# A Fourier mixing kernel: the place of column 128, the queues of the first batch's rows, and the order of the start-up

## The chip, the cores and the metric

The kernel runs on one NeuronCore of a Trainium2 chip. The metric is the device time of one execution in microseconds (us). The core's engines are PE (TensorE, with its weight loads as PEld), DVE (VectorE), ACT (ScalarE), POOL (GpSimd) and SP (SyncE, which here issues DMAs); each runs its own instructions in order and waits for the others by semaphores. DMAs are issued from the queues of SP, ACT and POOL and share 16 DMA engines.

## The reference

```python
def _attn_ref(x):                        # x: 8 batches x 3136 rows x 256 columns
    X = np.fft.fft(x, axis=1)
    X = np.fft.fft(X, axis=2)
    return X.real.astype(np.float32)

def _moe_ref(x, U, V, w_ch1, w_ch2):     # U 3136x32, V 32x3136, w_ch1 256x1024, w_ch2 1024x256
    xt = x.transpose(0, 2, 1)
    h = xt @ U @ V
    u = x + h.transpose(0, 2, 1)
    ch = np.maximum(u @ w_ch1, 0.0) @ w_ch2
    return (u + ch).astype(np.float32)
```

The second function gets the output of the first as its `x`. The kernel multiplies in bf16 and adds up in float32.

## The kernel before

**Folds and tables.** A batch's 3136 rows are loaded as four quarters of 784 rows, each twice: `xr` holds straight rows (`load_r`, a plain DMA), `xf` the rows in reversed order of partitions (`load_f`, an indirect DMA, a gather, from POOL). 98 partitions hold four rows of a quarter each, and one more partition holds row 0 of the quarters (`load_0`). DVE folds them. `along_d` subtracts (part 0) or adds (part 1) column 256 - d to column d, from float32 to bf16, into `EOF_` and `EOR_`; `alone` (POOL) copies the two columns without a partner, 0 and 128. `mirror` then joins straight and reversed rows (`EOS`), `half` makes `GO` (odd rows) and `GE` (even rows) out of that, and `fourth` makes the two `GC` out of `GE`. In these tiles a row has 258 columns of meaning: 0 to 127 are the sine part, 128 to 257 the cosine part. Before the change column 0 of `x` lies at 128, the cosines at 129 to 255, column 128 of `x` at 256, and zeros at 0 and 257. `GO` and `GC` are 384 columns wide (`GW`); `zeros` (POOL) clears 258 to 383 once.

**The transform on PE.** `products` lists matmuls whose weights are 128 columns of `GO` or `GC` (type 0: from column 0; type 1: from column 128) and whose moving operand is a strip of a table of sines or cosines (`TABO`, `TABS`, `TABE`), 196 to 424 columns long. To type 0 come the products of column 128 of `x`: the weights are columns 256 to 383, that is one column of data, the rest zeros. They add into the same PSUM tile. `u_odd` and `u_alone` list the same for the low-rank part, with strips of 32 columns. `seq` and `even_rows` run such a list into a PSUM tile `pt`; `chan`, `first_rows` and `first_u` then transform along the columns with the tables `MSN`, `MC` and `MSX` (a copy of `MSN` with another row 0).

**The network.** `direct` multiplies chunks of 512 rows of the result (`u`) by the first weights, with ReLU on ACT; `mirrors` makes the hidden values of the mirrored rows from those; `second_product` multiplies by the second weights and `store` writes the output. The rows of all batches are taken as 25 such chunks. While a chunk runs, the folds and the transform of a later batch are put between its steps (`due`, `turn`), by hand-written places. Behind L1178 the order of each engine's instructions is pinned for PE and for the folds.

**The start-up.** Up to L1178 the order is written by hand, per engine. POOL makes index rows by iota and issues the gathers. DVE computes phases; ACT makes sines and cosines. `flip_u` turns U's rows round by a matmul with `J`, `fold_u` folds them, and `transform_u` multiplies the folded U by the tables: `odd_k` and `even_k` on PE, into the PSUM tiles `pu`, and `evict` on ACT, which copies the result next to the tables. `filler` gives PE matmuls whose result nobody reads (`fill(n)` of them). The first batch is folded and transformed in two halves, sine and cosine: `half(0, 1, ...)`, `seq(0, 1, 0, ...)`, `seq_both` for the sine half (L1075 to L1087), then the same for the cosine half (L1096 to L1108). Between them POOL's gathers of batch 1 and `places` (the tile `EM`, L283) are issued. `setup.close()` (L1113) gives back the memory of the start-up tiles (`gen`), and the next tile, `u` of `first_u`, takes its place; `lrow`, which `EM` is made from, is among the start-up tiles. `first_u` and `direct(0, 0)` (L1153) follow.

## Time and profile before

| | us |
|---|---|
| median of 3 runs | 437.86 |
| lowest and highest of them | 437.59, 438.01 |
| profiled execution, its own time | 437.52 |
| its span, first instruction to last | 435.7 |
| granted TensorE clock in it | 1.0 |

A profile is one execution. A row of a timeline gives start, duration, engine, line, operation, the tile written and those read, and how many were merged; in brackets the idle time ahead of it and what ended that. A merged row's duration goes from the first start to the last end. Matmuls are pipelined, so one starts long ahead of the end of the one before it, and ends are modelled: for the pace of PE read the starts. `128*8` at a matmul means weights of 128 rows and 8 columns. A row of busy time by stretch has the stretch, its length, then busy time and number for PE, PEld, DVE, ACT and POOL, the granted clock, the share of DMA and GB/s. A row of the chain of waits has start, duration and what ran.

Nearly all instructions of helpers have the helper's line: L453 are folds on DVE, L463 matmuls, L57 gathers.

### The profile page before, as it was taken

What the parts mean: (1) busy time and instruction counts of PE and PEld (TensorE: products, weight loads), DVE (VectorE), ACT (ScalarE), POOL (GpSimd) and SP (SyncE); (2) the same over time, 40 slices, a digit from 0 to 9 for tenths busy, and PEclk for the clock granted to TensorE, in tenths of its full rate; (3) what the DMA queues carried; (4) which work ended last, traced back from release to release, by engine and by line L of the source; (5) the groups of instructions that cost most, each with busy time, mean ns of one, the idle gap of its engine ahead of it and who ended that gap; (6) DMA issues with size and microseconds to landing.
All of it is one profiled execution on the core that took longest, in us unless ns stands there. A gap on an engine that the chain in (4) does not pass through costs nothing.

```text
span 435.7 us, 9397 instructions
## 1 busy us (share of the span) xinstructions
PE 423.2 (97%) x3504; PEld 284.1 (65%) x3504; DVE 319.7 (73%) x665; ACT 291.7 (67%) x633; POOL 128.8 (30%) x340
## 2 busy tenths in 40 slices
PE   5989999999999999999999999999999999999996
PEld 2764667566766766666766766666666766666675
DVE  8988989797898787769777787779867554353442
ACT  7958775666667657776667657776667657765651
POOL 8971323142334223324233232322223101011111
PEclk9999999999999999999999999999999999999999
DMA  7898698868689486837886395866225323334543
GB/s 207 211 212 202 148 284 112 202 160 234 148 162 272 101 210 173 202 74 192 171 208 171 86 232 53 211 164 146 74 80 144 99 74 107 93 122 120 122 125 121
DMA packets 89165, 67.83 MB, mean 156 GB/s; under 512 B 55402, under 2 KB 82430, under 8 KB 89118
## 3 DMA queue, kind: packets, MB, share of 16 engines
q1 hardware_dynamic: 83350, 52.79, 51.3%
q0 software_dynamic: 5472, 14.36, 13.0%
q8 instruction: 27, 0.44, 0.4%
q14 instruction: 20, 0.16, 0.1%
q10 hardware_dynamic: 296, 0.07, 0.1%
HBM read 28.86 MB, written 25.69 MB: 125 GB/s over the span
## 4 chain that ended last, share of the span: by engine, by line
PE 79%; DVE 7%; DMA 7%; POOL 2%; ACT 2%; issue 1%; SPq 0%; ACTq 0%; DVEq 0%; POOLq 0%
PE p L463 65%; PE pt L463 7%; PE pst L463 4%; DMA out_dram<-o 3%; DMA xf<-in_x_dram,xidx 2%; DVE eof L453 2%; PE ph L463 2%; DVE eor L453 2%; DMA ut<-u 2%; POOL xf L57 1%; DVE u L458 1%; ACT h L843 1%; PE ptt L463 1%; DVE eos L453 1%; ACT h L859 1%
## 5 line engine op out<-in xcount | busy, mean ns | idle before, releaser
L463 PE MATMUL p<-w,h 128*128 128x256 bf16 x1576 | 195.2, 273 | 0.0
L463 PEld LDWEIGHTS <-h 128*128 128x128 bf16 x1576 | 148.6, 98 | 39.7 <-issue 15.8
L859 ACT ACTIVATE h<-p 128x512 bf16<-128x512 f32 (+1 forms) x200 | 101.5, 595 | 84.3 <-PE p L463 82.1
L843 ACT ACTIVATE h<-p 128x512 bf16<-128x512 f32 (+1 forms) x200 | 101.7, 599 | 8.0 <-PE p L463 7.6
L463 PE MATMUL p<-u,w 128*128 128x512 bf16 (+1 forms) x400 | 93.1, 375 | 1.3 <-ACT h L859 0.8
L921 DVE TENSOR_TENSOR o<-p,ut 128x256 f32<-128x256 f32 (+1 forms) x95 | 39.6, 417 | 68.1 <-PE p L463 47.2
L926 POOL TENSOR_TENSOR o<-o,fx 128x2 f32<-128x2 f32 (+1 forms) x95 | 40.6, 428 | 157.2 <-DVE o L922 82.5
L463 PEld LDWEIGHTS <-w 128*128 128x128 bf16 x512 | 41.7, 97 | 38.5 <-issue 2.5
L463 PE MATMUL p<-uo,wd 128*128 128x512 bf16 (+1 forms) x200 | 50.8, 375 | 0.2
L458 DVE TENSOR_TENSOR u<-ph,T 128x512 bf16<-128x512 f32 (+23 forms) x63 | 34.3, 556 | 9.6 <-PE ph L463 7.5
L57 POOL DMA_INDIRECT xf<-in_x_dram,xidx x32 | 36.8, 1150 | 11.3 <-issue 6.7
L922 DVE TENSOR_TENSOR o<-p,ut 128x256 f32<-128x256 f32 (+1 forms) x95 | 38.9, 410 | 0.0
L453 DVE TENSOR_TENSOR eof<-xf 99x1016 bf16<-99x1016 f32 (+1 forms) x33 | 38.4, 1173 | 0.5 <-DMA xf<-in_x_dram,xidx 0.5
L453 DVE TENSOR_TENSOR eor<-xr 99x1016 bf16<-99x1016 f32 (+1 forms) x34 | 38.4, 1145 | 0.0
L458 DVE TENSOR_TENSOR u<-ph,S 128x512 bf16<-128x512 f32 (+23 forms) x63 | 34.3, 555 | 0.8 <-PE ph L463 0.3
L817 POOL TENSOR_TENSOR fx<-ut 128x4 f32<-128x4 bf16 x48 | 16.4, 341 | 55.2 <-DMA ut<-u 55.2
L463 PEld LDWEIGHTS <-wd 128*128 128x128 bf16 x200 | 19.4, 98 | 13.0 <-issue 0.4
L463 PE MATMUL pt<-te,gc 98*128 98x229 bf16 (+1 forms) x192 | 24.0, 260 | 0.8 <-ACT ev L616 0.5
L463 PEld LDWEIGHTS <-gc 98*128 98x128 bf16 x216 | 19.4, 97 | 4.9 <-issue 1.1
L668 ACT CAST T<-pst 128x392 bf16<-128x392 f32 (+1 forms) x28 | 17.3, 618 | 6.9 <-PE pst L463 6.5
L463 PEld LDWEIGHTS <-go 98*128 98x128 bf16 x216 | 16.3, 97 | 6.7 <-issue 0.7
L668 ACT CAST S<-pst 128x392 bf16<-128x392 f32 (+1 forms) x28 | 17.5, 623 | 4.5 <-PE pst L463 4.4
(179 smaller groups left out, 449.7 us busy)
## 6 DMA issues: line engine op xcount, KB each, us to landing
out_dram<-o SPq DMA_DIRECT2D x33, 512.0 KB
xr<-in_x_dram SPq DMA_DIRECT2D x15, 784.0 KB
out_dram<-o SPq DMA_DIRECT2D x8, 384.0 KB
out_dram<-o SPq DMA_DIRECT2D x8, 256.0 KB
out_dram<-o SPq DMA_DIRECT2D x10, 128.0 KB
xr<-in_x_dram SPq DMA_DIRECT2D x2, 392.0 KB
ut<-u SPq DMA_TRANSPOSE x48
vv<-vv SPq DMA_DIRECT2D x3, 196.0 KB
```

Of the source, the lines that this page charges most:

```text
L57: nc.gpsimd.indirect_dma_start(out_, None, bass.AP(t.tensor, t.offset, [[w, rows], [1, w]]), bass.IndirectOffsetOnAxis(idx, 0), element_of ...
L453: ins = nc.vector.tensor_tensor(*a, **k)
L458: ins = nc.vector.tensor_tensor(*a, **k)
L463: ins = nc.tensor.matmul(*a, **k)
L668: eng(to, pt[:, :n])
L817: nc.gpsimd.tensor_tensor(fx[:, :, 1], ut[:, 0:n, 0] if hf else ut[:, n:2 * n, 0], ut[:, n + 1:2 * n + 1, 0], op=AL.subtract)
L843: nc.scalar.activation(k["h", 0][q][:, j - 4 * q, :w], p1[:, :w], AF.Relu)
L859: nc.scalar.activation(k["h", 1][q][:, g, :w], k["p1"][g][:, :w][:, ::-1], AF.Relu)
L921: nc.vector.tensor_tensor(o[:, ts, 0:P], p2[:, :w, 0:P], ut[:rows, ts, 0:P], op=AL.add)
L922: nc.vector.tensor_tensor(o[:, ts, P:D], p2[:, :w, P:D], strip(ut[:rows], (CH // P + t0 + 1) * P, [[P, w], [-1, P]]), op=AL.add)
L926: nc.gpsimd.tensor_tensor(o[:, ts, cols], o[:, ts, cols], fx[:rows, ts, 1 - hf:], op=AL.add)
```

## The change

Column 128 of `x` moves to column 128 of the folded tiles, next to the sine columns, with a zero at 129; column 0 moves to 130 and the cosines to 131 to 257. Its products take two columns of weights (128 and 129) and write two rows of PSUM. `GO` and `GC` are 258 columns wide, and `zeros` is gone. The first batch's sine half is folded in one operation over columns 0 to 129 for `GO`, `GE` and each `GC`, where there were two.

In the start-up, `J` is made in one operation and `pf` in two matmuls; the even phases are one operation instead of two. On SP's queue the straight quarters 1 and 3 go first; quarters 0 and 2 move to POOL's queue, between the gathers. `evict` is split, and its copies stand behind all of `transform_u`'s matmuls; the sines of `MSN` and `MC`, which stood ahead of them on ACT, follow behind. The fillings change from 20, 16, 15 to 20, 17, 12. The copy to `MSX`, with POOL's two memsets of it, moves from ahead of the first batch's products to behind its sine half. One fold of the last batch is due later.

```diff
-GW = 384
+GW = 258
+COL = (0, 130, 128)
...
-    iota(krow[:, 2 * NT:4 * NT], [[-2, 2 * NT]], 783)
+    iota(krow[:, 2 * NT:4 * NT], [[-NT, 2], [-2 * NT, 2], [-2, NT // 2]], 783)
...
     f0, r0, r3 = load_0(x, xf, xr, 0, D)
+    load_r(x, xr, 0, 1, 2, D)
     r0()
-    load_r(x, xr, 0, 1, 2, D)
     r3()
     f0()
-    for q in (0, 2):
-        load_r(x, xr, 0, q, 1, D)
-    iota(jv[:], [[1, KP]], 0, 1)
+    iota(jv[:, 0:PQ], [[1, PQ]], 0, 1)
+    iota(jv[:, PQ:KP], [[0, 1]], -1, 1)
     for q in (0, 2):
         load_f(x, xf, 0, q, D)
...
-    for q in (1, 3):
-        load_f(x, xf, 0, q, D)
+    load_r(x, xr, 0, 0, 1, D, nc.gpsimd)
+    load_f(x, xf, 0, 1, D)
+    load_r(x, xr, 0, 2, 1, D, nc.gpsimd)
+    load_f(x, xf, 0, 3, D)
...
-    def zeros(eng, s):
-        eng.memset(GO[s].rearrange("p a i d -> p (a i) d")[:, :, 258:GW].bitcast(I32), 0)
-        for c in range(2):
-            eng.memset(GC[s][c][:, :, 258:GW].bitcast(I32), 0)
...
-        for part, src in ((slice(0, NT), strip(krow[:KP], NT // 2, [[NT, 2], [1, NT // 2]])),
-                          (slice(NT, 2 * NT), krow[:KP, 3 * NT:4 * NT])):
-            dst = y[:, part].bitcast(FP32)
...
+        nc.vector.tensor_scalar(y.bitcast(FP32).rearrange("p (a j) -> p a j", a=4),
+                                strip(krow[:KP], NT // 2, [[NT, 4], [1, NT // 2]]), col, float(2 ** (23 - 15)),
+                                op0=AL.mult, op1=AL.add)
...
         nc.vector.tensor_single_scalar(J[:], jv[:], 97.0, op=AL.is_equal)
-        nc.vector.scalar_tensor_tensor(J[:], jv[:], 196.0, J[:], op0=AL.is_equal, op1=AL.add)
         pf = psum.tile([KP, 4, NI, R], FP32, tag="p1", name="pf", bufs=BUFS["p1"])
-        nc.tensor.matmul(pf.rearrange("p q i r -> p (q i r)"), J[:],
-                         UA.rearrange("p q i r -> p (q i r)"), start=True, stop=True)
+        for q in range(2):
+            nc.tensor.matmul(pf[:, q:4:2].rearrange("p q i r -> p q (i r)"), J[:],
+                             UA[:, q:4:2].rearrange("p q i r -> p q (i r)"), start=True, stop=True)
...
-            fold_tt(dst[:, qs, :, 129:256], lo, hi, op=AL.add)
+            fold_tt(dst[:, qs, :, 131:258], lo, hi, op=AL.add)
...
-        (eng or nc.gpsimd.tensor_copy)(dst[:, qs, :, 128:257:128], src[:, qs, :, 0:129:128])
+        (eng or nc.gpsimd.tensor_copy)(dst[:, qs, :, 130:127:-2], src[:, qs, :, 0:129:128])
...
+    def some(grp):
+        return slice(COL[grp], COL[grp] + (2 if grp == 2 else P))
...
-                    mm.append((at, g[:kp(i), i, col:col + P], TABE[t][:kp(i), i, lo:hi]))
+                    mm.append((at, g[:kp(i), i, cols], TABE[t][:kp(i), i, lo:hi]))
...
-            mm(pt[:, at:at + rhs.shape[-1]], w, rhs, start=(n == 0), stop=(n == len(todo) - 1),
+            mm(pt[:w.shape[-1], at:at + rhs.shape[-1]], w, rhs, start=(n == 0), stop=(n == len(todo) - 1),
                skip_group_check=True)
...
-            todo = todo + products(b, par, 1, 256, (pn == 1) == (par == 1), ne)
+            todo = todo + products(b, par, 1, 2, (pn == 1) == (par == 1), ne)
         elif typ == 0 and pn == 1:
-            todo = todo + [(QW, w, rhs) for w, rhs in u_odd(b, 1, 256)]
+            todo = todo + [(QW, w, rhs) for w, rhs in u_odd(b, 1, 2)]
...
-    zeros(nc.gpsimd, 0)
-    zeros(nc.gpsimd, 1)
...
-    sine(MSN[:, 0:128], pd[:, 0:128], 17, -1)
-    sine(MSN[:, 128:256], pd[:, 128:256], 17, 1)
-    cosine(MC[:], pd[:], 17)
-    msr = MSN[0:1].rearrange("p (l two) -> p l two", two=2)
...
-    nc.gpsimd.memset(msr[:, :, 0:1], 1.0)
-    nc.gpsimd.memset(msr[:, :, 1:2], -1.0)
...
     us[1]()
     uc[1]()
-    fill(16)
+    fill(17)
     us[0]()
     uc[0]()
+    us[3]()
+    uc[3]()
     us[2]()
     uc[2]()
+    sine(MSN[:, 0:128], pd[:, 0:128], 17, -1)
+    sine(MSN[:, 128:256], pd[:, 128:256], 17, 1)
+    cosine(MC[:], pd[:], 17)
+    msr = MSN[0:1].rearrange("p (l two) -> p l two", two=2)
+    nc.gpsimd.memset(msr[:, :, 0:1], 1.0)
+    nc.gpsimd.memset(msr[:, :, 1:2], -1.0)
+    fill(12)
+    half(0, 1, slice(0, 130))
+    seq(0, 1, 0, 0, "dft", False)
+    seq(0, 1, 0, 1, "p1")
+    nc.scalar.copy(W1[:, 1, :], w1t[:])
+    sin_odd = dict(ST[0])
+    half(0, 0, slice(0, 130))
+    for c in range(2):
+        fourth(0, c, slice(0, 130))
+    U0 = {}
+    seq_both(0, 0, "p1", lambda: u_alone(0, 0, U0))
+    sin_even = dict(ST[0])
     nc.scalar.copy(MSX[:], MSN[:])
     msr = MSX[0:1].rearrange("p (l two) -> p l two", two=2)
     nc.gpsimd.memset(msr[:, :, 0:1], -1.0)
     nc.gpsimd.memset(msr[:, :, 1:2], 1.0)
-    fill(15)
-    for cols in (slice(0, 128), slice(256, 258)):
-        half(0, 1, cols)
-    seq(0, 1, 0, 0, "dft", False)
-    seq(0, 1, 0, 1, "p1")
-    nc.scalar.copy(W1[:, 1, :], w1t[:])
...
-    mirror(1, slice(128, 256), AL.add)
-    half(0, 1, slice(128, 256))
+    mirror(1, slice(130, 258), AL.add)
+    half(0, 1, slice(130, 258))
...
-                                    (1, 2, 3, 5, 5, 5, 7.75, 8, 10, 11, 12, 13, 14, 15, 17))]
+                                    (1, 2, 3, 5, 5, 5, 7.75, 8, 10.75, 11, 12, 13, 14, 15, 17))]
```

More of the change, by code (lines that the diff above doesn't have):

```diff
@@ L163 @@
     for t in (EOF_, EOR_):
-        nc.vector.memset(t.rearrange("p a i d -> p (a i) d")[:, :, 0:258:257], 0.0)
+        nc.vector.memset(t.rearrange("p a i d -> p (a i) d")[:, :, 0:130:129], 0.0)
     GO = [cpool.tile([KP, 2, NI, GW], BF16, name=f"go{s}", tag=f"go{s}") for s in range(2)]
@@ L212, in phase_even @@
         y, col = phe[:, i // 2], ncol[:KP, i:i + 1]
-        for part, src in ((slice(0, NT), strip(krow[:KP], NT // 2, [[NT, 2], [1, NT // 2]])),
-                          (slice(NT, 2 * NT), krow[:KP, 3 * NT:4 * NT])):
-            dst = y[:, part].bitcast(FP32)
-            if part.start == 0:
-                dst = dst.rearrange("p (a j) -> p a j", a=2)
-            nc.vector.tensor_scalar(dst, src, col, float(2 ** (23 - 15)), op0=AL.mult, op1=AL.add)
+        nc.vector.tensor_scalar(y.bitcast(FP32).rearrange("p (a j) -> p a j", a=4),
+                                strip(krow[:KP], NT // 2, [[NT, 4], [1, NT // 2]]), col, float(2 ** (23 - 15)),
+                                op0=AL.mult, op1=AL.add)
         nc.vector.tensor_single_scalar(y, y, 2 ** 15 - 1, op=AL.bitwise_and)
@@ L245, in flip_u @@
         nc.vector.tensor_single_scalar(J[:], jv[:], 97.0, op=AL.is_equal)
-        nc.vector.scalar_tensor_tensor(J[:], jv[:], 196.0, J[:], op0=AL.is_equal, op1=AL.add)
         pf = psum.tile([KP, 4, NI, R], FP32, tag="p1", name="pf", bufs=BUFS["p1"])
-        nc.tensor.matmul(pf.rearrange("p q i r -> p (q i r)"), J[:],
-                         UA.rearrange("p q i r -> p (q i r)"), start=True, stop=True)
+        for q in range(2):
+            nc.tensor.matmul(pf[:, q:4:2].rearrange("p q i r -> p q (i r)"), J[:],
+                             UA[:, q:4:2].rearrange("p q i r -> p q (i r)"), start=True, stop=True)
         return pf
     def fold_u(UF):
-        for t in range(2):
-            op = AL.add if t else AL.subtract
-            nc.vector.tensor_tensor(uy[:, t, 0].rearrange("p a (i r) -> p a i r", r=R),
-                                    UF[:, 0:4:2], UR[:, 3::-2, ::-1], op=op)
-            nc.vector.tensor_tensor(uy[:, t, 1].rearrange("p a (i r) -> p a i r", r=R),
-                                    UR[:, 0:4:2, ::-1], UF[:, 3::-2], op=op)
+        for n in range(2):
+            for t in range(2):
+                two = (UR[:, 0:4:2, ::-1], UF[:, 3::-2]) if n else (UF[:, 0:4:2], UR[:, 3::-2, ::-1])
+                nc.vector.tensor_tensor(uy[:, t, n].rearrange("p a (i r) -> p a i r", r=R), *two,
+                                        op=AL.add if t else AL.subtract)
         nc.vector.tensor_tensor(GUO.rearrange("p t n i r -> p (t n) (i r)"),
@@ L362, in odd_k, with evict_even @@
                 fill(2)
-        def evict():
+        def evict_even():
             pu = PU[t]
@@ L369, in evict, with evict_odd @@
                                  pu[:KP, 6:8, :].rearrange("p c r -> p (c r)"), AF.Copy, scale=hv[:KP])
+        def evict_odd():
+            pu = PU[t]
             nc.scalar.copy(TABO[t].rearrange("p n i w -> p (n i) w")[:PQ, :, 2 * NT:WO], pu[:PQ, 8:12, :])
@@ L373, in evict @@
                                  AF.Copy, scale=hv[:KP])
-        return even_k, odd_k, evict
+        return even_k, odd_k, evict_even, evict_odd
     def both(t, i, c0, c1, step, n):
@@ L439, in half @@
         if par and b:
-            ins = nc.vector.tensor_copy(dst[:, :, :, 0], dst[:, ::-1, :, 256])
+            ins = nc.vector.tensor_copy(dst[:, :, :, 0], dst[:, ::-1, :, 128])
             if len(pinned) > 1:
@@ L509, in four, with products @@
         return strip(t, at, [[0, P // R], [1, R]])
-    def products(b, par, t, col, odd, ne):
-        mm = []
+    def some(grp):
+        return slice(COL[grp], COL[grp] + (2 if grp == 2 else P))
+    def products(b, par, t, grp, odd, ne):
+        mm, cols = [], some(grp)
         if par == 0:
@@ L526, in products, with u_odd @@
                 for nm in range(2):
-                    mm.append((at, GO[b % 2][:kp(i), nm, i, col:col + P],
+                    mm.append((at, GO[b % 2][:kp(i), nm, i, cols],
                                tab[:kp(i), nm, i // 2, lo:lo + n]))
         return mm
-    def u_odd(b, t, col):
+    def u_odd(b, t, grp):
         todo = []
@@ L535, in u_odd @@
             tab, lo = (TABS[t], off_u(t, i)) if i % 2 else (TABO[t], 2 * NT)
-            todo += [(GO[b % 2][:kp(i), nm, i, col:col + P], tab[:kp(i), nm, i // 2, lo:lo + NE])
+            todo += [(GO[b % 2][:kp(i), nm, i, some(grp)], tab[:kp(i), nm, i // 2, lo:lo + NE])
                      for nm in range(2)]
@@ L550, in seq @@
         d["pt"] = pt
-        todo = products(b, par, typ, P * typ, pn == 1, ne)
+        todo = products(b, par, typ, typ, pn == 1, ne)
         if typ == 0 and b == 0:
-            todo = todo + products(b, par, 1, 256, (pn == 1) == (par == 1), ne)
+            todo = todo + products(b, par, 1, 2, (pn == 1) == (par == 1), ne)
         elif typ == 0 and pn == 1:
-            todo = todo + [(QW, w, rhs) for w, rhs in u_odd(b, 1, 256)]
+            todo = todo + [(QW, w, rhs) for w, rhs in u_odd(b, 1, 2)]
         add_up(pt, todo)
@@ L607, in even_rows @@
         pt = d["pe"]
-        todo = products(b, 0, typ, P * typ, pn == 1, ne)
+        todo = products(b, 0, typ, typ, pn == 1, ne)
         if typ == 0:
-            todo = todo + products(b, 0, 1, 256, pn == 0, ne)
+            todo = todo + products(b, 0, 1, 2, pn == 0, ne)
         for n, (at, w, rhs) in enumerate(todo):
-            mm(pt[:, at:at + rhs.shape[-1]], w, rhs, start=(pn == 0 and n == 0),
+            mm(pt[:w.shape[-1], at:at + rhs.shape[-1]], w, rhs, start=(pn == 0 and n == 0),
                stop=(n == len(todo) - 1), skip_group_check=True)
@@ L644, in u_alone @@
         todo = []
-        for t, col in ((1, P),) if typ else ((0, 0), (1, 256)):
+        for t, col in ((1, 1),) if typ else ((0, 0), (1, 2)):
             for c in range(2):
@@ L648, in u_alone @@
                 lo = TE - NT + NE * c
-                todo += [(g[:kp(i), i, col:col + P], TABE[t][:kp(i), i, lo:lo + NE]) for i in range(NI)]
+                todo += [(g[:kp(i), i, some(col)], TABE[t][:kp(i), i, lo:lo + NE]) for i in range(NI)]
             todo += u_odd(b, t, col)
         for n, (w, rhs) in enumerate(todo):
-            mm(kept["pt"][:, typ, :], w, rhs, start=(n == 0), stop=(n == len(todo) - 1))
+            mm(kept["pt"][:w.shape[-1], typ, :], w, rhs, start=(n == 0), stop=(n == len(todo) - 1),
+               skip_group_check=True)
         nc.scalar.copy(ST[b]["tab"][:, typ, 0, :].rearrange("p (g r) -> p g r", r=R),
@@ L963, in spread @@
     def spread(t, i):
-        return ([(both(t, i, 0, 0, 1, NT), 0, 2 * NT), (TABO[t][:, 0, i // 2, 0:2 * NT], 2 * NT, 4 * NT)]
+        return ([(both(t, i, 0, 0, 1, NT), 0, 2 * NT),
+                 (strip(TABO[t][:, 0, i // 2, :], 0, [[NT // 2, 2], [NT, 2], [1, NT // 2]]), 2 * NT, 4 * NT)]
                 if i % 2 == 0 else
@@ L968, in spread, with piece @@
                  (TABS[t][:, 0, i // 2, off_t(t, i):off_t(t, i) + NT], NT, 2 * NT)])
-    def piece(y, lo, hi, two):
-        return y[:, lo:hi].rearrange("p (c j) -> p c j", c=2) if two else y[:, lo:hi]
+    def piece(y, lo, hi, out_):
+        n = len(out_.shape)
+        return (y[:, lo:hi] if n == 2 else y[:, lo:hi].rearrange("p (c j) -> p c j", c=2) if n == 3 else
+                y[:, lo:hi].rearrange("p (a c j) -> p a c j", a=2, c=2))
     def sines(i):
@@ L975, in sines @@
         for n, (out_, lo, hi) in enumerate(spread(0, i)):
-            sine(out_, piece(y, lo, hi, n == 0), 15, 1)
+            sine(out_, piece(y, lo, hi, out_), 15, 1)
     def cosine_even(i):
@@ L981, in cosine_even @@
         for n, (out_, lo, hi) in enumerate(spread(1, i)):
-            nc.scalar.activation(out_, piece(ab, lo, hi, n == 0), AF.Sin,
+            nc.scalar.activation(out_, piece(ab, lo, hi, out_), AF.Sin,
                                  scale=TWO_PI / 2 ** 15, bias=c_nhp[:KP])
@@ L1058 @@
     mirror(1, slice(0, 128), AL.subtract)
-    mirror(1, slice(256, 258), AL.add)
+    mirror(1, slice(128, 130), AL.add)
     fill = filler()
@@ L1073 @@
     nc.gpsimd.memset(msr[:, :, 1:2], 1.0)
-    fill(15)
-    for cols in (slice(0, 128), slice(256, 258)):
-        half(0, 1, cols)
-    seq(0, 1, 0, 0, "dft", False)
-    seq(0, 1, 0, 1, "p1")
-    nc.scalar.copy(W1[:, 1, :], w1t[:])
-    sin_odd = dict(ST[0])
-    for cols in (slice(0, 128), slice(256, 258)):
-        half(0, 0, cols)
-        for c in range(2):
-            fourth(0, c, cols)
-    U0 = {}
-    seq_both(0, 0, "p1", lambda: u_alone(0, 0, U0))
-    sin_even = dict(ST[0])
     for g in range(1, 4):
@@ L1100 @@
     cos_odd = dict(ST[0])
-    half(0, 0, slice(128, 256))
+    half(0, 0, slice(130, 258))
     for c in range(2):
-        fourth(0, c, slice(128, 256))
+        fourth(0, c, slice(130, 258))
     apart(0, 1, sin_odd)
```

## The prediction, made before the changed kernel ran

> **What bounds the kernel now.** I read the page's first part, then busy time by stretch, then the waits of PE behind the start-up.

> ```profile
> span 435.7 us, 9397 instructions
> PE 423.2 (97%) x3504; PEld 284.1 (65%) x3504; DVE 319.7 (73%) x665; ACT 291.7 (67%) x633; POOL 128.8 (30%) x340
> ...
> 100.00:150.00 50.00, 50.00 (x415) 33.71 (x413) 41.03 (x83) 34.69 (x76) 16.60 (x44) 1.00 0.82 188
> ...
> 400.00:420.00 20.00, 20.00 (x158) 13.58 (x156) 8.63 (x20) 12.58 (x27) 2.87 (x17) 1.00 0.50 121
> ...
> PE p L463 <- ACT h L859: 0.8, 1, 0.8
> ```

> The second figure of a stretch is PE: busy for all of its 50 and of its 20 us, at granted clock 1.00 (the last figure but two); DVE, two further on, is busy for 41 of 50. Behind 36 us its longest wait is 0.8 us. So from about 36 us on every nanosecond added to PE's stream is added to the end, and what VectorE (DVE) saves there is worth nothing. Ahead of that the chain of waits tells what sets the point from which PE runs full:

> ```profile
> 25.30 0.71 DVE eos L453
> 26.11 1.46 POOL xf L57
> 27.88 2.17 POOL xf L57
> ...
> 30.44 1.42 POOL em L283 x2
> ...
> 32.07 0.73 ACT u L723
> 32.85 0.38 PE p L463
> ```

> DVE's folds (`eof`, `eos`), then POOL (GpSimd) with two gathers of batch 1 and EM, and only then the copies of `u` (L721, L723), with which the first big product starts at 32.85. `u` lies in memory that the start-up pool gives back at L1113, and EM (L283) is the last POOL reader of a tile there (`lrow`).

> ```profile
> 31.59 0.40 PE L463 MATMUL psu<-vv,ta 32*128 32x256 bf16 x4
> ```

> PE's own last matmul for `u` ends at 31.59 + 0.40 = 31.99, EM at 30.44 + 1.42 = 31.86. Two chains end within 0.13 us of each other, so either one alone, made later, moves the start of the stream.

> **Two-column weights.** The products of column 128 load 2 weight columns instead of 128. As many columns stream past them, so their own length stays. What the trace has of narrow weights is the end of the last product, with 8 columns between two runs of 128:

> ```profile
> 428.02 1.04 PE L463 MATMUL p<-w,h 128*128 128x256 bf16 x8
> ...
> 428.98 1.04 PE L463 MATMUL p<-w,h 128*8 128x256 bf16 x8
> ...
> 429.96 0.83 PE L463 MATMUL p<-w,h 128*128 128x256 bf16 x6
> ```

> One of these takes 273 ns from its start to its modelled end, so starts inside a run of eight are (1.04 - 0.273) / 7 = 0.110 us apart, for 8 columns as for 128: narrow weights load in time. But eight steps are 0.877 us, and from the wide run to the narrow one go 0.96 us, from the narrow to the wide 0.98. Entering costs 0.08 to 0.09, leaving 0.10: 0.19 us for a narrow run between wide ones. Weights of 32 rows show the same:

> ```profile
> 58.10 0.38 PE L463 MATMUL ph<-vv,ta 32*128 32x512 bf16 x2
> 58.40 0.83 PE L463 MATMUL p<-w,h 128*128 128x256 bf16 x6
> ```

> From the `ph` products to the next wide one go 0.30 us where a 512-column product, at the pace above, needs 2 x 0.110 = 0.22.

> [...]

> In the order of the changed program there are 26 such runs between wide ones: 5 in the first batch, 3 in each of the seven others (both halves of the even rows, and the eight 32-column matmuls of the low-rank part). Seven batches: 21 x 0.19 = **+4.0 us** on PE. [...] Upper bound: the 8 x 7 short matmuls. Wide ones go at a 25 ns pace, (0.35 - 0.177) / 7 from the row `ptu` x8 below with 177 ns for one; if narrow loads went unhidden there, at about 86 ns each, they would add 56 x 0.061 = 3.4. I take 4.0, as the narrow run of eight loses nothing inside. Of the 0.8 us wait a part may swallow the three runs of batch 1; I take off 0.3 (bounds 0 and 0.6, all that batch 1 adds).

> ```profile
> L463 PEld LDWEIGHTS <-h 128*8 128x8 bf16 x8 | 0.6, 86 | 0.3 <-issue 0.2
> L463 PE MATMUL ptu<-te,gc 98*128 98x32 bf16 x18 | 1.0, 177 | 0.0
> ...
> 25.14 0.35 PE L463 MATMUL ptu<-te,gc 98*128 98x32 bf16 x8
> ```

> [...] The 25 ns pace of `ptu` with 128 columns says that loads are hidden; no gain is taken.

> **The front, DVE.**

> ```profile
> 1.56 0.49 DVE L206 TENSOR_SCALAR pho<-krow,ncol 99x392 f32<-99x392 f32 x1
> 2.08 0.36 DVE L208 TENSOR_SCALAR pho<-pho 99x392 int32<-99x392 int32 x1
> 4.90 0.26 DVE L246 SCALAR_TENSOR_TENSOR jx<-jv,jx 99x99 f32<-99x99 f32 x1
> 5.08 0.55 DVE L218 TENSOR_SCALAR phe<-krow,ncol 99x196 f32<-99x196 f32 x2
> 5.66 0.37 DVE L219 TENSOR_SCALAR phe<-phe 99x392 int32<-99x392 int32 x1
> ...
> 13.69 2.36 DVE L453 TENSOR_TENSOR eof<-xf 99x1016 bf16<-99x1016 f32 x2 [0.47 <-DMA xf<-in_x_dram,xidx]
> ...
> 21.61 0.78 DVE L453 TENSOR_TENSOR go<-eos 99x1024 bf16<-99x1024 bf16 x2
> 22.30 0.69 DVE L453 TENSOR_TENSOR ge<-eos 99x1024 bf16<-99x1024 bf16 x1
> 23.70 0.17 DVE L453 TENSOR_TENSOR ge<-eos 99x16 bf16<-99x16 bf16 x1
> 24.06 1.21 DVE L453 TENSOR_TENSOR eof<-xf 99x1016 bf16<-99x1016 f32 x1
> ```

> Steps are start to start. L246 gone: 5.08 - 4.90 = 0.18. Two `phe` pairs (0.58) become one operation of 392 (0.52 by `pho`): 2 x 0.06. Then the 0.47 us wait for the second gather. It must land 0.8 us earlier for the wait to go, at 12.9. Two of the four straight quarters leave the queue that moves beside it and come behind it on its own, so I take the wait as gone; bound, the gather lands as before, the wait stays and takes the 0.30 with it. The two-column folds of `go`, `ge` and `gc` merge into the wide ones: 0.09 from (22.30 - 21.61) less 0.60, and 24.06 - 23.70 = 0.36. Together `go` is ready about 0.9 earlier, and `eof` starts 0.18 + 0.12 + 0.47 + 0.09 + 0.36 = 1.2 earlier. The two straight quarters moved to POOL now stand behind the first two gathers, ahead of one other gather each; the bytes are the same and the folds of `eof` (2.36) and `eos` come ahead of their use, so 0 there (bound: one fold pair late, 1 us). Their issue costs POOL some 0.6 us each (L1040 below, a direct load), and jv has one iota more ahead of the gathers; this pushes back hv and the lone columns behind them, and the dropped memsets of zeros, which stood ahead of the lone columns, give it back.

> **The front, PE.**

> ```profile
> 22.45 0.84 PE L463 MATMUL pt<-ts,go 98*128 98x196 bf16 x8
> ...
> 25.90 0.20 PE L463 MATMUL ptu<-ts,go 99*128 99x32 bf16 x2
> 26.43 0.85 PE L463 MATMUL pt<-te,gc 98*128 98x197 bf16 x8 [0.33 <-ACT ev L616]
> 27.12 0.50 PE L463 MATMUL pt<-ts,go 98*128 98x196 bf16 x4
> ```

> Twelve filling matmuls for sixteen let PE follow DVE: first product at 21.55. To 27.12 it needed 4.67 us, of which 26.43 - 25.95 = 0.48 was the wait for the copy L616; that copy stood behind the MSX copy, which moves away. With 4.5 switch pairs (0.86) the sine part ends at 21.55 + 4.67 - 0.48 + 0.86 = 26.6, 0.5 earlier than before. PE alone would have its last `psu` 0.5 earlier, at 31.5.

> **What goes the other way: MSX.** Its copy moves behind the first batch's even sine rows, and POOL's two memsets of MSX with it; in POOL's order both still stand ahead of the last two gathers and EM.

> ```profile
> 24.25 0.41 ACT L1070 COPY msx<-msn 128x256 bf16<-128x256 bf16 x1 [2.34 <-POOL msn L1049]
> ...
> 27.55 0.38 ACT L620 CAST B<-pt 128x196 bf16<-128x196 f32 x1
> ...
> 18.46 0.59 POOL L1040 DMA_DIRECT2D w<-in_moe_w_ch_dram  x1
> ...
> 22.77 1.06 POOL L57 DMA_INDIRECT xf<-in_x_dram,xidx  x1 [0.30 <-issue]
> ...
> 24.72 0.24 POOL L1072 MEMSET msx<- 1x128 bf16 x1 [0.49 <-ACT msx L1070]
> 24.87 0.23 POOL L1073 MEMSET msx<- 1x128 bf16 x1
> ```

> The `B` copy ended at 27.93; 0.5 earlier is 27.4. MSX takes 0.41: 27.8. The memsets, 24.72 to 25.10, take 0.38: 28.2. The third gather of batch 1 starts at about 28.35, not 26.11. From there to EM's end the trace has 31.86 - 26.11 = 5.75 us: `u` at 34.15, 2.1 later than 32.07. With gathers as short as 1.06 (they ran beside a busy DVE, which is now done at about 29.8), 5.75 - (1.46 + 2.17) + 2 x 1.06 = 4.24: 32.6, or 0.5 later. I take **+0.9**, nearer the short ones; bounds 0.5 and 2.1. Behind `u` wait ACT's and DVE's copies and all of PE's stream.

> **Nothing on the path.** POOL's dropped memsets of zeros, flat `gc` and `go` folds in later batches (DVE at 41 of 50 us there, PE's stream covers them), the split `pf` (DVE comes to it with other folds), U's copies and the sines behind them on ACT: ACT stood idle for the 2.34 us ahead of MSX, and that covers them. Without this cover the copy of the first odd rows would come late by what is missing, and L616 with it, 0.48 at most as now.

> **Sum.** 4.0 - 0.3 + 0.9 = +4.6. The profiled execution took 437.52 us, 1.8 around its span, 0.34 under the median of 437.86: 442.1 beside it, **442.4 us** as a median.

> **Rivals.** (1) Narrow runs are free: 437.9 + 0.9 = 438.8. For it: no row has 2 columns; against: the 8-column row. (2) EM does not hold `u`, PE does: -0.5 + 3.7 gives 441.1. For it: PE's chain ended last by 0.13 us; against: the chain of waits runs through POOL. (3) Faster: DVE's shorter front carries through to the stream, with its 1.2 us, 436.7; it decides only if a narrow run costs under 1.2 / 21 = 0.06 us, a third of the row, and MSX is no gate. (4) Short narrow matmuls lose the hidden load: +3.4, 445.8; the pace inside the run of eight is against it. (5) A straight quarter on POOL's queue comes late: the front slips by up to 1 us, 443.4.

> **How the numbers follow.** Forecast 0.60, rival (1) 0.12, (2) 0.13, (3) 0.05, (4) 0.05, (5) 0.05. The forecast's own range is 441.7 to 443.9 (0.5 to 2.1 in front, 3.4 to 4.0 behind). With (2), (5) and an error of the switch price: 440.0 to 445.0. A measurement tells 0.2%, 0.9 us, from no change: (1) is split about its edge, so slower 0.90, same 0.05, faster 0.05.

> **What would show it.** Switches: two-column runs with some 0.1 us more ahead of and behind them, PE from 36 us to the end 4 us longer. MSX: the third and fourth gather from 28 us, `u` at 32.6 to 34, released by EM. DVE: no wait ahead of `eof`, `go` at 21.4. I am wrong if PE's stretch behind the first big product is as long as before, or if that product starts at 32.4 or earlier.

## The result, and the profile after

| | before | changed |
|---|---|---|
| median, us | 437.73 | 443.4 |
| lowest and highest, 6 runs each | 436.69, 438.65 | 442.4, 445.49 |
| profiled execution, its own time | 437.52 | 445.49 |
| its span | 435.7 | 443.7 |
| granted clock over the whole profile | 1.0 | 0.992 |

The ratio is 1.0134, 95% interval 1.0105 to 1.0163: slower by 5.7 us. The profiled execution is the slowest of its six, so it shows more loss than the median has. Ratios, here and below, leave out an execution that took over 1.5% longer than the fastest of its kernel; that is one, in e12. The first part of the page:

```profile
span 443.7 us, 9385 instructions
...
PE 431.6 (97%) x3504; PEld 281.6 (63%) x3504; DVE 318.7 (72%) x658; ACT 293.0 (66%) x633; POOL 128.4 (29%) x337
```

PE runs as many matmuls as before and is busy 8.4 us longer (431.6 for 423.2), the span being 8.0 longer. DVE has seven operations fewer; its share fell from 73% to 72%. Busy time by stretch tells two of the places:

```profile
30.00:32.00 2.00, 0.97 (x8) 0.55 (x6) 1.29 (x3) 1.01 (x4) 1.66 (x4) 0.98 1.03 244
32.00:34.00 2.00, 2.00 (x13) 0.98 (x12) 0.05 (x1) 0.09 (x1) 1.72 (x6) 0.50 1.04 219
36.00:38.00 2.00, 2.00 (x6) 0.68 (x5) 0.67 (x2) 1.49 (x3) 0.94 (x1) 0.50 0.96 209
38.00:40.00 2.00, 2.00 (x13) 1.29 (x12) 0.53 (x1) 1.47 (x4) 0.00 (x0) 0.82 0.89 201
400.00:420.00 20.00, 20.00 (x151) 12.94 (x150) 8.65 (x20) 12.39 (x24) 2.43 (x15) 1.00 0.46 115
```

The last figure but two is the granted clock: from 32 to 38 us PE runs at half. If it is either full or half, the means of the stretches beside it (0.98 and 0.82) put the ends at 31.9 and 38.7. In the last row PE is as busy as before, at full clock, with 151 matmuls in 20 us for 158; the two stretches lie some 8 us of work apart, so the counts only point to a slower stream, and its steps show it. This is the timeline of PE at a two-column run of batch 1:

```profile
75.09 0.20 PE L458 MATMUL pt<-ts,go 98*2 98x32 bf16 x2
75.14 0.20 PE L458 MATMUL pt<-to,go 98*2 98x32 bf16 x2
75.19 0.20 PE L458 MATMUL pt<-ts,go 99*2 99x32 bf16 x2
75.32 1.06 PE L458 MATMUL pt<-te,gc 98*128 98x229 bf16 x8
```

Inside the run two matmuls take 0.05 us, the 25 ns pace of wide ones. Behind the last two the next wide one could start at 75.24; it starts at 75.32. Over the whole profile, by the starts of neighbouring matmuls less the time that the first one streams, the 21 steps from 128 columns to two cost 93.7 ns on average, the 21 steps back 92.9, and the 91 steps inside narrow runs 0.5. One run costs 0.187 us, 21 of them 3.9 us.

The start-up, as the timeline of several engines has it:

```profile
28.20 0.42 ACT L1085 COPY msx<-msn 128x256 bf16<-128x256 bf16 x1
...
28.68 0.23 POOL L1087 MEMSET msx<- 1x128 bf16 x1 [4.39 <-ACT msx L1085]
...
29.46 1.06 POOL L58 DMA_INDIRECT xf<-in_x_dram,xidx  x1 [0.40 <-issue]
30.82 0.95 POOL L58 DMA_INDIRECT xf<-in_x_dram,xidx  x1 [0.30 <-issue]
...
31.43 1.01 PE L458 MATMUL psu<-A,mc 128*128 128x256 bf16 x4 [0.98 <-PE ptt L458]
...
32.13 1.45 POOL L275 TENSOR_SCALAR em<-lrow,hm 128x128 bf16<-128x128 f32 x2
...
33.22 0.61 PE L458 MATMUL psu<-vv,ta 32*128 32x256 bf16 x4
...
33.91 0.73 ACT L723 CAST u<-psu 128x512 bf16<-128x512 f32 x1 [2.09 <-PE psu L458]
...
34.68 3.57 PE L458 MATMUL p<-u,w 128*128 128x512 bf16 x8 [0.31 <-ACT u L723]
```

POOL stands for 4.39 us before MSX's memsets, and the third and fourth gather of batch 1 start at 29.46 and 30.82 instead of 26.11 and 27.88. EM ends at 33.58. PE ends `psu` at 33.83, for it ran most of these twelve matmuls at half clock. `u` starts at 33.91, 1.84 later than before, and the first big product at 34.68 for 32.85. Its eight matmuls take 3.57 us from first start to last end; the same row of the run of the changed kernel shown below, at full clock, has 1.89.

So the 8.0 us of this profile are 1.8 in front of the first big product, 1.8 to 1.9 of half clock behind it, 3.9 of switches, and some 0.4 more. Of these, 0.26 lie behind PE's last matmul: from its end to the end of the span go 4.01 us, where the kernel before has 3.75.

DVE's front:

```profile
12.75 2.33 DVE L448 TENSOR_TENSOR eof<-xf 99x1016 bf16<-99x1016 f32 x2
...
15.96 0.70 DVE L448 TENSOR_TENSOR eos<-eof,eor 99x1040 bf16<-99x1040 bf16 x1 [0.28 <-POOL eof L420]
...
20.19 0.69 DVE L448 TENSOR_TENSOR eof<-xf 99x508 bf16<-99x508 f32 x1 [0.49 <-DMA xf<-in_x_dram,xidx]
...
21.72 0.70 DVE L448 TENSOR_TENSOR go<-eos 99x1040 bf16<-99x1040 bf16 x1
```

`eof` starts 0.94 earlier than before (12.75 for 13.69), and `go` ends at 22.42 where it ended at 22.39. On the way DVE waited 0.28 us for POOL's lone columns and 0.49 for the fourth gather, waits that were not there before.

### The profile page after: what moved, and what is told of

It reads as the page before. It is cut to its first block, busy times and chain, and to the rows that moved or that the text cites. A ratio compares the mean times of both kernels' runs of the same rounds, so it can differ in the third digit from the quotient of the medians.

```text
span 443.7 us, 9385 instructions
## 1 busy us (share of the span) xinstructions
PE 431.6 (97%) x3504; PEld 281.6 (63%) x3504; DVE 318.7 (72%) x658; ACT 293.0 (66%) x633; POOL 128.4 (29%) x337
## 4 chain that ended last, share of the span: by engine, by line
PE 90%; DMA 4%; ACT 2%; DVE 2%; issue 1%; ACTq 0%; SPq 0%; DVEq 0%
PE p L458 68%; PE pt L458 9%; PE pst L458 4%; PE fill L1020 3%; PE ph L458 2%; DMA ut<-u 2%; DMA qf<-qt 1%; PE ptt L458 1%; ACT h L859 1%; ACT h L843 1%; PE pu L314 1%; DMA ua<-in_moe_U_dram 1%; PE psu L458 1%; PE pq L458 1%; DVE eor L448 1%
## 5 line engine op out<-in xcount | busy, mean ns | idle before, releaser
L859 ACT ACTIVATE h<-p 128x512 bf16<-128x512 f32 (+1 forms) x200 | 101.6, 593 | 86.3 <-PE p L458 84.1
L458 PE MATMUL p<-u,w 128*128 128x512 bf16 (+1 forms) x400 | 94.8, 380 | 1.2 <-ACT h L859 0.9
L453 DVE TENSOR_TENSOR u<-ph,T 128x512 bf16<-128x512 f32 (+23 forms) x63 | 34.3, 556 | 9.6 <-PE ph L458 7.6
L453 DVE TENSOR_TENSOR u<-ph,S 128x512 bf16<-128x512 f32 (+23 forms) x63 | 34.2, 554 | 0.8 <-PE ph L458 0.3
L817 POOL TENSOR_TENSOR fx<-ut 128x4 f32<-128x4 bf16 x48 | 15.8, 328 | 61.1 <-DMA ut<-u 61.0
L458 PE MATMUL pt<-te,gc 98*128 98x229 bf16 (+3 forms) x192 | 25.5, 260 | 0.4 <-DVE u L453 0.2
L458 PEld LDWEIGHTS <-gc 98*128 98x128 bf16 (+1 forms) x216 | 17.0, 92 | 8.3 <-issue 4.2
L816 POOL TENSOR_TENSOR fx<-ut 128x4 f32<-128x4 bf16 x24 | 7.3, 306 | 51.4 <-DMA ut<-u 51.4
L458 PEld LDWEIGHTS <-go 98*128 98x128 bf16 (+1 forms) x216 | 15.0, 92 | 9.1 <-issue 4.1
```

The source lines that it names most:

```text
L453: ins = nc.vector.tensor_tensor(*a, **k)
L458: ins = nc.tensor.matmul(*a, **k)
L817: nc.gpsimd.tensor_tensor(fx[:, :, 1], ut[:, 0:n, 0] if hf else ut[:, n:2 * n, 0], ut[:, n + 1:2 * n + 1, 0], op=AL.subtract)
L859: nc.scalar.activation(k["h", 1][q][:, g, :w], k["p1"][g][:, :w][:, ::-1], AF.Relu)
```

## The experiments

Columns, start-up and clock are taken apart in this order. "Before" beside each is the kernel before in the same session.

**e1: the changed kernel again.**

> The changed kernel once more, for a second profile. In the first one 21 two-column runs behind the front took 0.19 us more each, 3.9 us in all, and the first big product began 1.8 us later than before and ran its first 3 us at half clock, which cost 1.9 us more. If the half clock belongs to the change (PE stands idle longer ahead of u), this profile shows it too and the median stays at +5 to +6 us; if it was a chance of that one execution, this profile is 1.5 to 2 us shorter than 443.7 with the clock at 1.0 there, and u is late all the same.

Measured: 445.3 us beside 437.88, ratio 1.0164 (1.0128 to 1.0199). This time the profile fell on an execution at full clock, span 442.5. POOL, ACT and PE in its timeline:

```profile
31.54 1.45 POOL L275 TENSOR_SCALAR em<-lrow,hm 128x128 bf16<-128x128 f32 x2
...
33.01 0.72 ACT L723 CAST u<-psu 128x512 bf16<-128x512 f32 x1 [1.80 <-POOL em L275]
...
33.79 1.89 PE L458 MATMUL p<-u,w 128*128 128x512 bf16 x8 [1.05 <-ACT u L723]
```

PE had ended `psu` at 32.41; `u` waited until 33.01, for EM's end at 32.98. So at full clock EM holds `u`, and the big product starts 0.94 late. The half clock is an addition that some executions have. It is not all that sets executions apart: the longest of these six, 446.76 us, has a granted clock of 1.0. Nor does this profile, 6.7 us longer than the one before, come down to the start (0.9) and the switches (3.9): PE waits 2.0 us for `h` (L859) in batch 1 where it waited 0.8, 0.26 lie at the end, and some 0.4 stay without a place.

**e2: two weight columns alone.** Columns 256 and 257 of the old layout, nothing else:

```diff
-                    mm.append((at, g[:kp(i), i, col:col + P], TABE[t][:kp(i), i, lo:hi]))
+                    mm.append((at, g[:kp(i), i, wide(col)], TABE[t][:kp(i), i, lo:hi]))
```

`wide` gives two columns where `col` is 256 and 128 elsewhere; the other places that list such weights are edited alike.

> The kernel before with one edit: column 128 keeps its place at 256, but its products load 2 weight columns (256, 257) instead of 128 and write 2 rows of PSUM. Switch theory: 21 runs behind the front at 0.19 us each, +4.0 us there, front within 0.3 us (PE has 0.5 us of waits there): +3.7 to +4.3 us. Rival, that the loss behind the front comes from the new place and pitch of the columns or from later waits: within 0.5 us of the kernel before.

Measured: 441.48 us beside 437.88, ratio 1.0082 (1.0064 to 1.01): +3.6. From the first big product to the end of the last copy of `o` its profile has 402.72 us for 399.83. The difference of 2.9 is 3.94 less 1.05 that batch 1 swallowed: PE's 0.8 us wait for `h` (L859) is gone from its waits. Narrow runs are not free. The front was expected within 0.3 us and is not: the first big product starts 0.97 late, at 33.82. The first batch has five two-column runs, 5 x 0.187 = 0.93, and here PE's `psu` (its end at 32.96) holds `u`, not EM (31.29). So the +3.6 is not the price of the 21 later runs alone.

**e6 and e7: 96 and 64 columns.** The same edit with 96 and with 64 for 2.

> The kernel before, with 96 weight columns in place of 128 for column 128 (two that count and 94 zeros). Theory (the price is that of a change between two configurations of the array, and 96 columns run in the same configuration as 128): no gap between wide and 96-column matmuls, 437.4 to 438.4 us, ratio within 0.998 to 1.002. Rival (any column count other than 128 loses the hidden weight load or the pairing, whatever the configuration): some 94 ns at each end of 21 runs as with two columns, ratio 1.007 to 1.010, 441 to 442 us.

> The kernel before, with 64 weight columns in place of 128 for column 128. Theory of the configuration (64 columns are another configuration than 128): the same 94 ns at each end of 21 runs as with two columns, +3 to +4 us, ratio 1.007 to 1.010. Rival (the price belongs to very narrow weights, two to thirty-two columns, and shrinks with the width): less than +1.5 us, ratio below 1.004.

Measured: 96 columns 438.58 us, ratio 1.0027 (1.0011 to 1.0043); 64 columns 442.02, ratio 1.0109 (1.0092 to 1.0126), both beside 437.16. At 64 columns the steps in and out cost 94.0 and 95.2 ns (means of 21), as for two. At 96 there is no such step: the one out of a 228-column matmul takes 101 ns where the matmul itself streams for 97.5. So the price has the pattern that the theory of configurations asks for: the same at 2 and at 64 columns, none at 96. What inside PE makes it no run shows. Both times lie above what was expected, e6's +1.4 and e7's +4.9, of which the steps make 4.0. The rest has another cause, weight loads, by form, first e6, then e7, then e2 (the last figure ahead of the second bar is ns for one):

```profile
L463 PEld LDWEIGHTS <-go 98*128 98x128 bf16 x108 | 9.7, 97 | 5.6 <-issue 1.1
L463 PEld LDWEIGHTS <-go 98*96 98x96 bf16 x54 | 4.0, 124 | 1.2
```

```profile
L463 PEld LDWEIGHTS <-go 98*64 98x64 bf16 x54 | 2.6, 111 | 3.0 <-issue 2.9
```

```profile
L463 PEld LDWEIGHTS <-go 98*2 98x2 bf16 x54 | 1.8, 81 | 3.1 <-issue 2.9
```

Loading 96 columns takes longer than loading 128 (124 ns for 97), and short matmuls show it: with 32 columns streaming, starts are 42.6 ns apart at 96 weight columns, 34.7 at 64, 25.2 at two. Forty-nine such steps lose 17.6 ns and seven more 20: 1.0 us of e6's 1.4. In e7 the same 49 steps and 28 of 229 columns (111.6 ns for 98) lose 0.9. Loading 64 columns, at 111 ns, also takes longer than loading 128; loading two, at 81 ns, takes less.

**e3: the shifted table early.** The changed kernel with

```diff
+    nc.scalar.copy(MSX[:], MSN[:])
...
     fill(12)
...
-    nc.scalar.copy(MSX[:], MSN[:])
```

(and its two memsets likewise).

> The changed kernel with the copy to MSX and its two memsets put back ahead of the first batch's products; all else as changed. Gate theory (POOL's last two gathers and EM stand behind the MSX memsets, and u waits for EM): gathers start at 25 to 26.5 us, u at 32 to 32.6, the big products begin 1.3 to 1.8 us earlier than in the changed kernel, at full clock, and the time falls by 1.5 to 3 us. Rival, that PE's own chain holds u: gathers earlier, but u and the time within 0.5 us of the changed kernel.

Measured: 442.32 us beside 437.88, ratio 1.0111 (1.0082 to 1.0141), 3.0 under e1 in the same session. EM ends at 30.86 and no longer matters; PE ends `psu` at 32.33 and `u` starts at 32.40. Of the front's loss 0.33 is left.

**e4: the old column layout with the rest of the change, and e8: the late table alone** in the kernel before.

> The changed kernel with the old places of the columns (0 and cosines from 128, column 128 of x at 256, 384 wide, weights of 128 columns, the memsets of zeros, two folds where the change has one); the front's new order, queues and the late MSX stay. Switch theory: the stretch behind the first big product is as long as before, the loss that is left is the front's 1 to 2 us: +1 to +2 us on the kernel before. Rival, that the pace behind the front is lost by other parts of the change: +4 us or more on the kernel before.

> The kernel before, with only the shifted table's copy and its two memsets moved behind the batch's fillings and sine products, as the change has them. Theory (the late table alone makes the front's loss): the third gather lands at 28.5 to 30 us, EM is the last operand of U's first product, which starts at 33 to 34 us on ACT (32.07 before); 439 to 441 us, ratio 1.002 to 1.007, more at the upper end if PE then runs its first big products at half clock. Rival (the table is hidden by the products' own chain): u within 0.3 us of before, ratio below 1.002.

Measured: e4 440.41 us beside 437.88, ratio 1.0049 (1.0032 to 1.0066), +2.5 where +1 to +2 were expected; e8 439.85 beside 437.16, ratio 1.0063 (1.0042 to 1.0083). POOL, ACT and PE, first e4, then e8:

```profile
32.60 1.45 POOL L281 TENSOR_SCALAR em<-lrow,hm 128x128 bf16<-128x128 f32 x2
...
34.09 0.73 ACT L729 CAST u<-psu 128x512 bf16<-128x512 f32 x1 [2.46 <-POOL em L281]
...
34.87 3.51 PE L464 MATMUL p<-u,w 128*128 128x512 bf16 x8 [1.71 <-ACT u L729]
```

```profile
31.95 1.45 POOL L283 TENSOR_SCALAR em<-lrow,hm 128x128 bf16<-128x128 f32 x2
...
33.43 0.73 ACT L723 CAST u<-psu 128x512 bf16<-128x512 f32 x1 [2.46 <-POOL em L283]
...
34.21 1.89 PE L463 MATMUL p<-u,w 128*128 128x512 bf16 x8 [1.71 <-ACT u L723]
```

In both EM releases `u`, and PE stands for 1.71 us ahead of it. In e4 the clock falls at 34.8, at the end of this gap, and the eight matmuls take 3.51; in e8's profile it does not. The late table alone makes 2.7 us, of which the profiled start shows 1.36; four of e8's six runs, at granted clocks of 0.995 and 0.996, average 440.5, the two at 1.0 average 438.85, which is 1.7 for the table without the clock. In e4, six of eight runs, at 0.996 or less, average 440.6 and the other two 439.3. Behind the first products e4 loses nothing: PE starts there 3.6 late and ends 3.84 late.

**e11 and e12: PE kept busy.** The changed kernel with filling matmuls behind the low-rank product and beside the spare product, e12 as below, e11 with eight of them behind `transposed` (`hold` adds as many matmuls as its second argument says, and nothing reads what they write):

```diff
+        if not b:
+            hold(pt[:, 320:512], 6)
...
+    hold(spare[:, 256:512], 7)
     transposed(0, spare)
```

> The changed kernel with 14 filling matmuls added on TensorE: 6 of 192 columns behind the low-rank product, 8 of 256 columns behind the spare product, where it waits for A and for U's first product. They write columns of PSUM that nothing reads. Theory (TensorE's idle stretches ahead of the late u drop the clock, which costs about 1.5 us in the runs where it happens): every run keeps a granted clock of 0.998 or more, the first eight p<-u,w take 1.5 us, and the median falls by 0.7 to 1.5 us below the changed kernel's (443.4 and 445.3 in two sessions) to 442 to 444 us. Rival (the clock falls for another reason, or idleness here does not matter): runs at 0.996 and below stay, the median is 443.5 us or more.

> The changed kernel with the 6 fillings of e11 behind the low-rank product, and 7 of 256 columns ahead of the spare product in place of the 8 behind it, so that they wait for no ACT copy and fall into the gap ahead of u. Theory (idle TensorE drops the clock): all runs at a granted clock of 0.998 or more, no gap over 0.7 us ahead of p<-u,w, p<-u,w starts with u and not later, and the median is 442.3 to 443.3 us, 1.5 to 2 us below the runs of the changed kernel and of e11 that show 0.996 or less (444.6 to 446.6). Rival (the clock falls whether TensorE is idle there or not): half of the runs or so at 0.996 or less again, median 443.5 to 445 us.

Measured: e11 444.0 us beside 437.64, ratio 1.0154 (1.013 to 1.0177); e12 442.17 beside 437.78, ratio 1.0084 (1.0059 to 1.011). PE in e11, then in e12:

```profile
34.60 1.03 PE L672 MATMUL spare<-to 98*128 98x256 bf16 x8 [1.53 <-ACT td L739]
35.47 1.89 PE L458 MATMUL p<-u,w 128*128 128x512 bf16 x8
```

```profile
33.57 0.94 PE L672 MATMUL spare<-to 98*128 98x256 bf16 x7
34.34 0.22 PE L458 MATMUL spare<-tab,msn 128*128 128x128 bf16 x1
...
35.26 1.89 PE L458 MATMUL p<-u,w 128*128 128x512 bf16 x7 [0.53 <-ACT u L730]
```

e11 missed its aim: its eight fillings waited for ACT's copy of `spare`, which comes behind `u`, so the gap stayed (1.53 us) and the fillings came ahead of the big product. Three of its six runs show 0.996 or less, on average 444.8 us, the others 443.0. In e12 the gap is 0.53, as before the change, and the big product starts with `u`; five of its six runs have clocks of 0.998 or more and take 441.3 to 442.7 us, the sixth has 0.977 and 451.3. The five are what the theory of idle time asks for. The changed kernel had 0.996 or less in 4 of its 12 runs, so five good runs support it and are too few to prove it.

Over all runs, 0.996 or less goes with the late table: 4 of 12 in the changed kernel, 6 of 8 in e4, 4 of 6 in e8, 3 of 6 in e11. With the table early it is 1 of 6 in e3, 1 of 12 in e5, none of 41 in e2, e6, e7, e9 and e10, and none of the 67 of the kernel before beside them. That the link is PE's idle time is argued: the profiles of e3 and e5, at full clock themselves, have gaps of 0.53 and 0.52 ahead of the big product, and still one run of each kernel was at the lower clock.

**e5, e9, e10: the loads.** e5 has the old columns and the early table, e9 the old loads besides, e10 only the two queues. This is e10's edit, but for the straight quarters 1 and 3, which go one place forward on SP's queue:

```diff
-    for q in (0, 2):
-        load_r(x, xr, 0, q, 1, D)
...
-    for q in (1, 3):
-        load_f(x, xf, 0, q, D)
+    load_r(x, xr, 0, 0, 1, D, nc.gpsimd)
+    load_f(x, xf, 0, 1, D)
+    load_r(x, xr, 0, 2, 1, D, nc.gpsimd)
+    load_f(x, xf, 0, 3, D)
```

> The changed kernel with the old column layout (128 weight columns, zeros behind) and with the shifted table's copy and its two memsets back ahead of the fold-in fillings; the front's fewer VectorE operations, the two queues for the straight rows and U's late copies stay. Theory (the time behind the front is only the switch of the array, the front's loss is only the late shifted table and the slow clock that the late u brings): the fourth gather lands by about 27.5 us, U's first product on ACT starts at 31.5 to 32.5 us at full clock, PE from there on as before, 437.0 to 438.5 us, ratio 0.998 to 1.002. Rival (the rest of the front loses by itself: straight rows on POOL's queue, POOL's slower copies): u at 33 us or later, 439 us or more with the table early too.

> The old column layout and the early shifted table as in e5, and the straight rows of the first batch loaded from one queue in the old order; of the change only the fewer VectorE operations and U's late copies are left. Theory (the two queues make e5's loss: VectorE, done earlier, waits for rows that land later): eof's fold of the cosine rows starts by about 13.3 us, and the run is 0.5 to 1.5 us shorter than e5 (438.68), at 437.0 to 438.2 us, ratio 0.998 to 1.002. Rival (U's copies or the fold-in fillings make it, or e5's loss is spread of the starts): within 0.4 us of e5, ratio 1.002 to 1.004.

> The kernel before, with only the straight rows of the first batch on two queues in the changed order. Theory (the two queues cost the front): the last gathers or the straight quarter land 0.5 to 1.5 us later, go's end moves from 22.3 us to 22.8 to 23.5 us, 437.8 to 439 us, ratio 1.001 to 1.004. Rival (the order of the loads is hidden by VectorE's folds): ratio 0.999 to 1.001.

Measured: e5 438.68 us beside 437.16, ratio 1.0027 (1.0008 to 1.0046); e9 437.75 beside 437.64, ratio 0.9995 (0.998 to 1.001); e10 437.71 beside 437.64, ratio 1.0013 (0.9998 to 1.0029). POOL in e5, then in e9:

```profile
8.36 0.62 POOL L77 DMA_DIRECT2D xr<-in_x_dram  x1
...
10.94 1.02 POOL L290 TENSOR_SCALAR hv<-ncol 128x1 f32<-128x1 f32 x1
...
15.68 1.25 POOL L426 CAST eof<-xf 99x16 bf16<-99x16 f32 x1
```

```profile
9.26 0.62 POOL L290 TENSOR_SCALAR hv<-ncol 128x1 f32<-128x1 f32 x1
...
14.06 1.30 POOL L426 CAST eof<-xf 99x16 bf16<-99x16 f32 x1
```

The two extra issues (0.62 us for the one shown) push POOL's own work back: `hv` from 9.26 to 10.94, the lone columns from 14.06 to 15.68. Where DVE comes to them, with the old zeros still ahead of them, it waits; these are rows of DVE in e4, then in e10:

```profile
17.49 0.70 DVE L454 TENSOR_TENSOR eos<-eof,eor 99x1040 bf16<-99x1040 bf16 x1 [1.80 <-POOL eof L426]
```

```profile
16.71 0.70 DVE L453 TENSOR_TENSOR eos<-eof,eor 99x1040 bf16<-99x1040 bf16 x1 [0.67 <-POOL eof L425]
```

In e5 itself DVE waited 1.44 us for a gather instead, so its start cannot be put down to these rows. Nor is that gather late by the queues alone: e9, with the old loads, has DVE idle ahead of the same fold, which was expected by 13.3 and began at 14.03:

```profile
14.03 2.36 DVE L454 TENSOR_TENSOR eof<-xf 99x1016 bf16<-99x1016 f32 x2 [1.20 <-issue]
```

By e5 against e9 the two queues cost some 1.4 us, by e10 0.6, with an interval that includes no change; there `go` ends at 22.55, not at 22.8 or later as expected. One part shows in every profile: from PE's last matmul to the end of the span go 3.98 to 4.01 us in the eight profiles with POOL's two loads, 3.75 in the six without. What e9 settles better is the other side: what it keeps of the change, `J` and the even phases in one operation each, `pf` in two matmuls, U's late copies and the sines behind them, is worth 0.9995, no difference that these runs can tell. No kernel here beats the one before.

## Why the prediction was right or wrong

**The bound.** Right. What PE's stream got, the end got; DVE's dropped operations changed nothing behind 36 us.

**Switches, +4.0.** Right, and for the reason given: 3.9 us in the profile, 3.94 in e2's stream, and by e7 and e6 64 columns pay the same price and 96 none. That two columns cost what eight do was the author's estimate: the row of eight, 0.19 us, was worth 0.187 at two. Rival (1), narrow runs free, is out, and with it rival (3), a faster kernel, which needed a run under 0.06. The upper bound, short narrow matmuls that lose the hidden load, is out at two columns (25.2 ns from start to start) and real at 96 (42.6). That two columns gain nothing by their shorter load holds: such a load has 81 ns for 97, and the 25 ns pace stays. What was not foreseen is that the five runs of the first batch reach `u` when EM does not hold it (0.97 in e2).

**The part swallowed in batch 1, 0.3.** In e2 it was 1.05, in the changed kernel nothing: its wait for `h` is 0.9 us, not 0.8. That wait stands behind a transposing DMA of `u` and varies by over 1 us from one profile to another (none in e10, 2.0 in e1), so the term was a guess inside its spread.

```profile
PE p L458 <- ACT h L859: 0.9, 1, 0.9
```

**DVE's front, `go` 0.9 earlier.** This step failed. `eof` came in time (12.9 worked out, 12.75 measured), but the prediction put two things behind it at nothing: the landing of the fourth gather, which it did not weigh, and POOL's lone columns, which the dropped memsets were to pay for. In the profile of the change these made DVE wait 0.49 and 0.28 and `go` ended as late as before. It is not the same in every profile: `go` ends at 21.83 in e1, where the gather was no limit, and at 22.23, 22.41 and 23.30 in e3, e11 and e12. Rival (5), a straight quarter on POOL's queue late by 1 us, had the queue right; a wait for a straight quarter shows in e12's profile alone, 0.42. With `go` not earlier, the steps that hung on it (first product at 21.55, `psu` ending at 31.5) failed too: 22.48 and 33.83, or 21.89 and 32.41 in e1. The last filling went from 15 matmuls to 12, not from sixteen as the prediction has it.

**MSX late, +0.9.** The mechanism was right, third gather and EM included (28.35 forecast; 28.87 in e1, 29.46 in the profile of the change), and e1's start of the stream, 0.94 late, is the term. In the profile of the change the last step was another: PE at half clock ended `psu` at 33.83, behind EM at 33.58, and released `u`. As time the term was too small: 2.7 us for the late table alone (e8), above the upper bound of 2.1, which had counted the wait and not the clock. Within a kernel the runs at the lower clock are longer by 1.3 (e4), 1.6 (e8), 1.8 (e11) and 2.0 us (444.9 against 442.9 in the changed one).

What makes the clock fall is argued, not shown. In the kernel before, PE's gaps ahead of `psu` and of the big product are 0.48 and 0.53 us:

```profile
30.41 0.82 PE L463 MATMUL psu<-A,mc 128*128 128x256 bf16 x4 [0.48 <-ACT A L620]
...
32.85 1.89 PE L463 MATMUL p<-u,w 128*128 128x512 bf16 x8 [0.53 <-ACT u L723]
```

A `u` held by EM stretches the second to 1.05 (e1) and 1.71 (e4, e8), and in e4 the clock falls at the end of it. In the profile of the change it fell at 31.9, in the middle of `psu` and ahead of `u`, so the wait for `u` cannot have made it fall there. The gap ahead of `psu` had grown too, to 0.98, but it is 0.96 in e1, whose clock stayed. That gap is 0.47 or 0.48 in e2, e3, e4 and e8; why it is longer in the changed kernel no run shows.

Rival (2), EM does not hold `u`, is out by e1, e4 and e8. With the table early PE does hold it (e2, e3).

**No cost elsewhere.** Split `pf`, U's copies, sines: right, by e9 and by e4's lossless stream behind the first products. Flat folds are in neither; for them speaks e3, where PE loses 4.0 us between the first big product and the end, what the switches cost. The two queues, by their issues taken as paid for, are the exception: 0.25 us at the end of the span, and a front that the runs do not settle.

**The sum.** +4.6 forecast, +5.7 measured here and +7.4 in e1's session. That 443.4 us lies in the forecast's range of 441.7 to 443.9 is in part luck, for the range had no term for the clock; e1's 445.3 lies outside. Alone, columns have 3.6 and the late table 2.7, but in front the two do not simply add up: both delay the same `u`, by 0.97 (e2, through PE) and 1.36 (e8, through EM). The forecast's distance is the clock's share, the DVE gain that did not come in full, and in e1 also the longer wait for `h`. Neither mark of being wrong appeared: from the first big product to the end of the last copy of `o` go 405.7 us for 399.8, of which 1.9 are the clock's, and that product starts at 34.7.

## What to carry to other kernels

On a PE that is never idle, fewer weight columns bought no time here, and runs of 2 and of 64 columns between wide ones paid the same 93 to 95 ns at each end: count such runs, not their columns, or put them next to each other. A step taken off one engine's path still has its place in another's order: POOL's gathers and EM stood behind the memsets of a table that nobody needed yet. An engine's wait ahead of a long stream may cost more than itself: with the table late (e12 aside) 17 of 32 runs had a lower clock, with the table early 2 of 126. Two savings or losses that end at the same wait do not add up.
